# A fused linear-attention and feed-forward kernel rebuilt with tokens on partitions, DMA transposes from the ninth chunk on, and an order written out by a planner

## The chip, the core and the metric

The kernel runs on one core of one Trainium2 chip. The metric is the device time of one launch in microseconds (us). A core has five engines that run their own instruction queues: TensorE (PE, with its weight loads shown apart as PEld), VectorE (DVE), ScalarE (ACT), GpSimd (POOL) and SyncE (SP, which here only issues transfers). Sixteen DMA engines move data. PSUM is the memory that TensorE writes; SBUF is the working memory, 128 partitions wide.

## The reference

Four inputs `r, k, v, w` have shape (4 batches, 8 heads, 768 steps, 48 channels); `u` is (8, 48). For each batch and head a 48 x 48 state runs over the steps, and a feed-forward layer of 384 to 2048 to 384 with a leaky ReLU follows on all 3072 tokens:

```
for t in range(S):
    cur   = outer(u * k[t], v[t])
    y[t]  = r[t] @ (state + cur)
    state = w[t][:, None] * state + outer(k[t], v[t])
x = y rearranged to (3072 tokens, 384)
h = x @ w_in                    # 384 x 2048
out = maximum(0.01 * h, h) @ w_out   # 2048 x 384
```

Everything comes and goes in float32; the inputs are 4 x 4.7 MB, the weights 2 x 3.1 MB and the output 4.7 MB.

## The kernel before, in words

The 768 steps of a batch are cut into 6 chunks of 128 tokens, so there are 24 chunks. In a chunk the recurrence is written as matrix products: the logs of `w` are summed along the tokens by a product with a triangular matrix, `r` and `k` are scaled with the exponentials of the sums, scores of all token pairs are formed and masked, and the state is carried from chunk to chunk. Two heads of 48 channels, padded to 64 each, share the 128 partitions: a pair. So a chunk has four pairs.

For each pair (loop over `p`) TensorE transposes `r` and `k` in float32 (L261, L269), forms the log sums with channels on partitions (L277), the scores of each head (L296), and then four products per head into one tile `ytsu` that has the channels on partitions: masked scores times `v` (L313), the `u` term as a product with the identity (L317), the carried state (L325, 64 rows) and the new state's sum (L332, 64 columns). ScalarE takes the exponentials (L285), VectorE scales and masks (L290, L303) and updates the state (L344). GpSimd and VectorE make `dk`, the `u` term's diagonal and `vsc` (L239 to L251). `ytsu` is copied into `xT`, in which each pair fills 112 of 128 rows.

After every third chunk a feed-forward block of 384 tokens is emitted (`mlp_block`): 16 groups of 4 products, one per pair, into `hp` (L149; two buffers), a copy on ScalarE (L157) and the leaky ReLU on VectorE (L159); then three sums of 16 products into `op` (L171), a copy and the store (L180). `w` is loaded per batch (L191), `r, k, v` per chunk (L212 to L220), all from SP; the weights come as casting transfers from GpSimd's queue (L128 to L135). The order on each engine is that of a tile scheduler, which works blocks and later chunks into one another.

Of the kernel before, what the change touches and what calls it, by code (L numbers as in the profile page):

```python
# [12 lines left out]
AX = mybir.AxisListType  # L13


@with_exitstack
def kernel(
# [11 lines left out]
    nc = tc.nc  # L29
    B, H, S, D = r.shape  # L30
    L = 128
    assert S % L == 0
    C = S // L
    assert H % 2 == 0
    NPAIR = H // 2
    assert D <= 48
    NH = H * D
    NT = NPAIR
    KROWS = 64 + D
    FF = moe_w_in.shape[1]  # L40
    assert FF % 128 == 0
    NFT = FF // 128
    NOUT = moe_w_out.shape[1]
    NTOK = B * S
    MB = 384
    assert S % MB == 0, "sequence must be multiple of mlp block"
    MBC = MB // L

    const = ctx.enter_context(tc.tile_pool(name="const", bufs=1))
    wpool = ctx.enter_context(tc.tile_pool(name="wpool", bufs=1))  # L50
    xtpool = ctx.enter_context(tc.tile_pool(name="xtpool", bufs=1))
    wbpool = ctx.enter_context(tc.tile_pool(name="wbpool", bufs=2))
    natpool = ctx.enter_context(tc.tile_pool(name="natpool", bufs=5))
    slabpool = ctx.enter_context(tc.tile_pool(name="slabpool", bufs=3))
    pairpool = ctx.enter_context(tc.tile_pool(name="pairpool", bufs=8))
    statepool = ctx.enter_context(tc.tile_pool(name="statepool", bufs=2))
    mlppool = ctx.enter_context(tc.tile_pool(name="mlppool", bufs=3))
    gtpool = ctx.enter_context(tc.tile_pool(name="gtpool", bufs=20))
    psum = ctx.enter_context(tc.tile_pool(name="psum", bufs=1, space=bass.MemoryType.PSUM))
    psum2 = ctx.enter_context(tc.tile_pool(name="psum2", bufs=2, space=bass.MemoryType.PSUM))  # L60

    ident_f = const.tile([128, 128], F32, name="ident_f")
    make_identity(nc, ident_f)
    ident_b = const.tile([128, 128], BF16, name="ident_b")
    make_identity(nc, ident_b)

    tcomb = const.tile([128, 256], BF16, name="tcomb")
    nc.gpsimd.memset(tcomb[:, 0:128], 1.0)
    nc.gpsimd.affine_select(
        out=tcomb[:, 0:128],  # L70
        in_=tcomb[:, 0:128],
        compare_op=ALU.is_gt,
        fill=0.0,
        base=0,
        pattern=[[1, 128]],
        channel_multiplier=-1,
    )
    nc.gpsimd.memset(tcomb[:, 128:256], -1.0)
    nc.gpsimd.affine_select(
        out=tcomb[:, 128:256],  # L80
# [41 lines left out]
    def load_weights():  # L122
        if weights_loaded[0]:
            return
# [263 lines left out]
```

## Time and profile before

| | us |
|---|---|
| median of 2 runs (390.86 to 392.42) | 391.64 |
| span of the profiled execution, first to last instruction | 385.2 |
| TensorE busy in the span | 337.2 (88%) |
| VectorE, ScalarE, GpSimd busy | 219.8, 161.4, 107.8 |

The profile is that of one execution, whose own time is its span of 385.2 us and what lies around it; no launch time is given for it, so the 6.4 us between its span and the median of the runs are taken for what lies around it. Busy times are those of a span, and a matmul's mean time is its latency: matmuls are pipelined, so a mean can be longer than the distance from one to the next.

### The profile page before, as it was taken

The page shows a single profiled execution, that of the slowest core. Times are in us where ns is not written, and L with a number is a line of the kernel's source. Part 1 is how long each engine was busy: PE and PEld are TensorE (multiplying, and loading weights), DVE is VectorE, ACT ScalarE, POOL GpSimd, SP SyncE. Part 2 cuts the span into 40 slices and gives each one's busy share as a digit, 9 for nine tenths or more (in the row PEclk, how much of TensorE's full clock was granted, in tenths as well). Part 3 has the DMA queues.
Part 4 walks back from the last instruction along what each step waited for, and adds up shares of the span by engine and source line. Part 5 has one row for each costly group of instructions (what it writes and reads, how often), then busy time and mean ns, then how long its engine had stood idle before and what let it go on. Part 6 is the DMA issues. An engine that isn't in the chain of part 4 may idle for free.

```text
span 385.2 us, 6034 instructions
## 1 busy us (share of the span) xinstructions
PE 337.2 (88%) x2136; PEld 187.8 (49%) x2136; DVE 219.8 (57%) x662; ACT 161.4 (42%) x382; POOL 107.8 (28%) x177
## 2 busy tenths in 40 slices
PE   0455169999999999999999999999999999999886
PEld 0232034455555555556555555555555655555343
DVE  0434045448656884767568837675588457724450
ACT  1535012343375633454486433542375235512341
POOL 5893055141152431234144303331331011000000
PEclk9999999999987999999999999999999999998699
DMA  7999999131532225212323233222220100010001
GB/s 159 176 205 227 217 166 167 15 64 20 128 57 54 39 57 115 48 21 53 96 42 58 57 93 60 41 43 82 43 41 3 62 2 0 2 61 3 0 0 63
DMA packets 87295, 27.33 MB, mean 71 GB/s; under 512 B 75489, under 2 KB 86881, under 8 KB 87265
## 3 DMA queue, kind: packets, MB, share of 16 engines
q1 hardware_dynamic: 84688, 23.80, 31.9%
q0 software_dynamic: 2576, 3.15, 4.8%
q8 instruction: 17, 0.28, 0.3%
q14 instruction: 14, 0.11, 0.1%
HBM read 25.36 MB, written 4.72 MB: 78 GB/s over the span
## 4 chain that ended last, share of the span: by engine, by line
PE 79%; SPq 7%; DMA 5%; DVE 5%; ACT 2%; issue 1%
PE hp L149 24%; PE op L171 16%; PE ytsu L325 7%; PE ytsu L332 6%; PE ytsu L313 6%; PE trcs L261 5%; PE mt L296 4%; DMA w_nat<-in_w_dram 4%; SPq L212 4%; PE trcs L269 3%; PE trcs L277 3%; PE ytsu L317 3%; DVE gt L159 2%; SPq L191 2%; PE esu_ps L227 1%; DVE vsc L251 1%
## 5 line engine op out<-in xcount | busy, mean ns | idle before, releaser
L149 PE MATMUL hp<-xT,w_in_b 112*128 112x384 bf16 x512 | 112.5, 347 | 8.6 <-DVE gt L159 7.0
L159 DVE SCALAR_TENSOR_TENSOR gt<-hp,hs 128x384 bf16<-128x384 f32 x128 | 70.1, 554 | 29.6 <-ACT hs L157 28.3
L157 ACT CAST hs<-hp 128x384 bf16<-128x384 f32 x122 | 58.3, 480 | 53.7 <-PE hp L149 52.3
L149 PEld LDWEIGHTS <-w_in_b 112*128 112x128 bf16 x512 | 50.2, 102 | 41.6 <-issue 18.7
L303 DVE TENSOR_TENSOR mtm<-mt,maskb 128x128 bf16<-128x128 f32 x192 | 51.2, 286 | 27.8 <-PE mt L296 27.1
L171 PE MATMUL op<-w_out_b,gt 128*128 128x384 bf16 x384 | 63.7, 326 | 0.4 <-DVE gt L159 0.4
L285 ACT ACTIVATE ef<-trcs 128x256 f32<-128x256 f32 x96 | 36.2, 384 | 47.6 <-PE trcs L277 45.3
L171 PEld LDWEIGHTS <-gt 128*128 128x128 bf16 x384 | 37.6, 98 | 25.0 <-issue 0.6
L313 PE MATMUL ytsu<-mtm,nat_v 128*64 128x128 bf16 x192 | 47.0, 255 | 1.3 <-DVE mtm L303 1.3
L239 POOL TENSOR_TENSOR dk<-nat_kf,esu 128x512 bf16<-128x512 f32 x24 | 27.8, 1157 | 71.7 <-ACT esu L235 71.3
L185 ACT CAST xT<-ytsu 128x128 bf16<-128x128 f32 x88 | 23.4, 266 | 51.0 <-PE ytsu L332 50.3
L261 PE MATMUL trcs<-ident_f,nat_rf 128*128 128x128 f32 x96 | 32.5, 338 | 13.1 <-DMA nat_rf<-in_r_dram 9.7
L317 PE MATMUL ytsu<-ident_b,vsc 128*64 128x128 bf16 x192 | 43.6, 236 | 0.0
L290 DVE TENSOR_TENSOR rka<-trcs,ef 128x256 bf16<-128x256 f32 x96 | 39.0, 408 | 4.7 <-ACT ef L285 4.7
L332 PE MATMUL ytsu<-nat_v,dk 128*64 128x64 bf16 x192 | 40.8, 222 | 0.0
L325 PE MATMUL ytsu<-rka,s_new 64*64 64x128 bf16 x160 | 40.3, 252 | 0.0
L313 PEld LDWEIGHTS <-nat_v 128*64 128x64 bf16 x192 | 20.2, 110 | 36.8 <-issue 28.8
L296 PE MATMUL mt<-rka 48*128 48x128 bf16 x192 | 28.4, 236 | 8.0 <-DVE rka L290 8.0
L241 POOL TENSOR_TENSOR t<-nat_rf,ukb 128x384 f32<-128x384 f32 x24 | 25.2, 1051 | 32.4 <-DMA nat_rf<-in_r_dram 32.3
L179 ACT COPY osb<-op 128x384 f32<-128x384 f32 x24 | 11.5, 479 | 52.5 <-PE op L171 52.5
L344 DVE SCALAR_TENSOR_TENSOR s_new<-s_new,atot,ytsu 128x64 bf16<-128x64 bf16 x80 | 21.9, 277 | 18.8 <-ACT xT L185 18.2
L251 DVE TENSOR_TENSOR vsc<-nat_vf,diag 128x512 bf16<-128x512 f32 x24 | 22.9, 956 | 14.3 <-PE ytsu L317 14.2
(47 smaller groups left out, 323.0 us busy)
## 6 DMA issues: line engine op xcount, KB each, us to landing
nat_rf<-in_r_dram SPq DMA_DIRECT2D x24, 192.0 KB, 3.2
nat_kf<-in_k_dram SPq DMA_DIRECT2D x24, 192.0 KB, 3.6
nat_vf<-in_v_dram SPq DMA_DIRECT2D x24, 192.0 KB, 2.9
out_dram<-osb SPq DMA_DIRECT2D x24, 192.0 KB, 1.9
w_in_b<-in_moe_w_in_dram POOLq DMA_DIRECT2D x8, 192.0 KB, 8.9
w_out_b<-in_moe_w_out_dram POOLq DMA_DIRECT2D x1, 1536.0 KB, 20.6
ukb<-in_u_dram SPq DMA_DIRECT2D x1, 192.0 KB, 3.6
w_nat<-in_w_dram SPq DMA_DIRECT2D x4, 0.2 KB, 16.3
```

The costliest lines, as they stand in the source:

```text
L149: nc.tensor.matmul(hp[:], lhsT=w_in_b[0:KROWS, t, j * 128 : (j + 1) * 128], rhs=xT[0:KROWS, t, T0 : T0 + MB], start=(t == 0), stop=(t == N ...
L157: nc.any.tensor_copy(out=hs[:], in_=hp[:])
L159: nc.vector.scalar_tensor_tensor(out=gt[:], in0=hp[:], scalar=0.01, in1=hs[:], op0=ALU.mult, op1=ALU.max,)
L171: nc.tensor.matmul(op[:], lhsT=gts[j][:, tsub * 128 : (tsub + 1) * 128], rhs=w_out_b[:, j, :], start=(j == 0), stop=(j == NFT - 1),)
L261: nc.tensor.matmul(trcs[:, 0:128], lhsT=nat_rf[:, hA : hA + 2, :].rearrange("p h d -> p (h d)"), rhs=ident_f[:], is_transpose=True, start= ...
L290: nc.vector.tensor_tensor(out=rka[:], in0=trcs[:, 0:256], in1=ef[:, 0:256], op=ALU.mult)
L296: nc.tensor.matmul(mt[:], lhsT=rka[r0 : r0 + D, 128:256], rhs=rka[r0 : r0 + D, 0:128], start=True, stop=True,)
L303: nc.vector.tensor_tensor(out=mtm[:, hi * 128 : (hi + 1) * 128], in0=mt[:], in1=maskb[:], op=ALU.mult,)
L313: nc.tensor.matmul(yap, lhsT=nat_v[:, hd, :], rhs=mtm[:, hi * 128 : (hi + 1) * 128], start=True, stop=False,)
L317: nc.tensor.matmul(yap, lhsT=vsc[:, hd, :], rhs=ident_b[:], start=False, stop=(s_prev is None),)
L325: nc.tensor.matmul(yap, lhsT=s_prev[r0 : r0 + 64, :], rhs=rka[r0 : r0 + 64, 0:128], start=False, stop=True,)
L332: nc.tensor.matmul(ytsu[r0 : r0 + 64, 128:192], lhsT=dk[:, hd, :], rhs=nat_v[:, hd, :], start=True, stop=True,)
```

## The change

The program is written anew. Tokens are on the partitions up to the output of a chunk; the feed-forward input is packed.

- **Recurrence.** A chunk is worked as a whole, not by pairs. One product (L332 of the changed kernel) gives the log sums of all heads with tokens on partitions; `ci`, `er`, `ek` and the scaled `rk` (r and k side by side, bf16, heads padded to 64) are made in 384 columns each. `rk` is then transposed to `rkT`: in chunks 0 to 7 by 8 bf16 products with the identity and two copies (L385 to L396), from chunk 8 on by one transposing transfer on SP (L402). Scores are 8 products of 48 rows (L471), masked by two VectorE operations of 512 columns (L494). The output `yp` has tokens on partitions: 4 products of the carried state for two heads at once (L522, 96 columns) and 8 of the masked scores (L526, 48 columns). The `u` term is no product any more: it is a GpSimd operation (L423) and an addition (L537). The state's sums are 4 products (L482). `y` is transposed into `xT` in 3 pieces of 128 rows: by products and a copy in chunks 0 to 7 (L547), by one transposing transfer from chunk 8 on (L559).
- **Chunk decay.** The factor for the carried state is made in chunks 1 to 7 by 4 products of one column (L337) and an exponential (L435). From chunk 8 on, row 0 of `er` goes to a scratch row in DRAM (L443), comes back spread over the partitions as 128 x 4 single values (L448), and VectorE takes the reciprocal (L453).
- **Feed-forward.** Blocks are of one chunk, 128 tokens. The 384 channels fill 3 full tiles of 128 rows: 48 products of 128 columns per chunk (L579), in groups of 12 into one `hp` tile of 512 columns (two of them), one leaky ReLU on ScalarE per group (L613), 16 products of 384 columns into the one `op` tile (L631), a copy on VectorE (L642) and the store (L646).
- **Weights** are loaded as float32 by SP in 8 pieces of 0.79 MB behind the first chunks' inputs, and cast by VectorE and ScalarE (L250 to L275).
- **Order.** `Plan` takes every step with an engine, a duration, its dependencies and a priority, and lists the steps by the start times that it finds; the program is emitted in this order on each engine. The recurrence's priorities are 10 per chunk, those of the feed-forward products 1000 and more, so feed-forward products stand where no step of the recurrence was ready.

```diff
-            for p in range(NPAIR):
-                ... (transposes, log sums, scores, four products per head, copies)
-            if (c + 1) % MBC == 0:
-                q = (b * S + (c + 1 - MBC) * L) // MB
-                mlp_block(q)
+    APE = 8
+    NPE = 8
+    LEAD = 3
+    AHEAD = 5
+    WEIGHTS = [(1, 4)] * 4 + [(3, 24)] * 4
+    hp_r = ring("hp", 2, [128, 512], F32, psum)
+    op_r = ring("op", 1, [128, DM], F32, psum)
...
+        for n in range(NCH):
...
+            for src, use in ((w, wn), (k, kn), (r, rn), (v, vn)):
+                def load(src=src, use=use, b=b, t0=t0):
+                    nc.sync.dma_start(
+                        out=use.t, in_=src[b, :, t0 : t0 + L, :].rearrange("h p d -> p h d")
+                    )
...
+            if n < NPE:
+                def tpose(rk=rk, trv=trv):
+                    for g in range(2 * NP):
+                        nc.tensor.transpose(
...
+            else:
+                s_T = [step(
+                    "SP", 0.6,
+                    lambda rk=rk, rkT=rkT: nc.sync.dma_start_transpose(
+                        out=rkT.t[:], in_=rk.t[:].rearrange("p a h d -> p (a h d)")),
...
+                    s_row = step(
+                        "SP", 0.45,
+                        lambda ad=ad, er=er: nc.sync.dma_start(
+                            out=ad.t[:], in_=er.t[0:1].rearrange("o h d -> o (h d)")),
...
+                    s_sp = step(
+                        "SP", 0.45,
+                        lambda ad=ad, a_in=a_in: nc.sync.dma_start(
+                            out=a_in.t[:], in_=ad.t[:].rearrange("o (p q) -> q (o p)", p=NP)),
...
+            def scores(rkT=rkT, se=se, so=so):
+                for p in range(NP):
+                    for par, sc in enumerate((se, so)):
+                        q0 = 64 * par
+                        nc.tensor.matmul(
+                            sc.t[:, p, :], lhsT=rkT.t[q0 : q0 + D, NP + p, :],
+                            rhs=rkT.t[q0 : q0 + D, p, :], start=True, stop=True, skip_group_check=True)
...
+                xt_steps.append(step(
+                    "SP", 0.6,
+                    lambda y=y, col=col: nc.sync.dma_start_transpose(
+                        out=xT[:, :, col : col + L], in_=y.t[:].rearrange("p h d -> p (h d)")),
...
+                def up(hp, j=j, J=J, N=N, c0=c0):
+                    for a in range(J):
+                        for t in range(KT):
+                            nc.tensor.matmul(
+                                hp.t[:, a * N : (a + 1) * N],
+                                lhsT=w_in_b[:, t, (j + a) * 128 : (j + a + 1) * 128],
+                                rhs=xT[:, t, c0 : c0 + N], start=(a == 0 and t == 0),
+                                stop=(t == KT - 1), skip_group_check=True)
...
+        for i in plan.order():
+            plan.fn[i]()
```

What the change does to the queues is seen in the order of the instructions. On TensorE before, the second head's products of a pair stand like this, each with its own weight load (`s_new` is the carried state, `dk` the decayed k):

```order
L317 LDWEIGHTS vsc
L317 MATMUL ytsu<-ident_b,vsc 64x128
L325 LDWEIGHTS s_new
L325 MATMUL ytsu<-rka,s_new 64x128
L332 LDWEIGHTS dk
L332 MATMUL ytsu<-nat_v,dk 64x64
```

In the changed kernel the same place of TensorE's queue, in chunk 12, holds the end of the state's sums and the scores, alternately for the upper and the lower half of the rows:

```order
L482 LDWEIGHTS rk_91
L482 MATMUL pp_150<-vb_99,rk_91 128x96
L471 LDWEIGHTS rkT_94
L471 MATMUL se_147<-rkT_94 128x128
L471 LDWEIGHTS rkT_94
L471 MATMUL so_148<-rkT_94 128x128
```

Between two such pieces stand the feed-forward groups, first products of 128 columns and then products of 384, each with a weight load of 128 columns:

```order
L579 LDWEIGHTS w_in_b
L579 MATMUL hp_144<-xT,w_in_b 128x128
L579 LDWEIGHTS w_in_b
L579 MATMUL hp_144<-xT,w_in_b 128x128
L631 LDWEIGHTS g_130
L631 MATMUL op_145<-w_out_b,g_130 128x384
L631 LDWEIGHTS g_130
L631 MATMUL op_145<-w_out_b,g_130 128x384
```

The products with 64 rows and those with the identity are gone from the steady part; the feed-forward's first products are 48 per chunk with a third of the columns each.

On SP's queue before, past the start, there are only loads and stores:

```order
L212 DMA nat_rf<-in_r_dram 128x8x48
L216 DMA nat_kf<-in_k_dram 128x8x48
L180 DMA out_dram<-osb 128x384
L220 DMA nat_vf<-in_v_dram 128x8x48
L180 DMA out_dram<-osb 128x384 x2
```

In the changed kernel the queue holds from chunk 8 on, per chunk, four loads, one store, the two transposing transfers and the two of the decay:

```order
L297 DMA in_74<-in_r_dram 128x8x48
L443 DMA ad_140<-er_87 1x512
L559 DMA_TRANSPOSE xT<-y_126 128x3x128
L297 DMA in_74<-in_v_dram 128x8x48
L402 DMA_TRANSPOSE rkT_96<-rk_92 128x8x128
L297 DMA in_75<-in_w_dram 128x8x48
L297 DMA in_75<-in_k_dram 128x8x48
L443 DMA ad_141<-er_85 1x512
L448 DMA a_118<-ad_140 128x4x1
```

Each transposing transfer stands in line with the loads of later chunks, and waits there for the VectorE operation that makes its source.

## Rows read from the trace of the kernel before

**Rows 1.** Page, parts 1 and 2: busy us; busy tenths in 40 slices.

```profile
PE 337.2 (88%) x2136; PEld 187.8 (49%) x2136; DVE 219.8 (57%) x662; ACT 161.4 (42%) x382; POOL 107.8 (28%) x177
PE   0455169999999999999999999999999999999886
```

**Rows 2.** Page, part 4: chain that ended last, share by engine and by line.

```profile
PE 79%; SPq 7%; DMA 5%; DVE 5%; ACT 2%; issue 1%
PE hp L149 24%; PE op L171 16%; PE ytsu L325 7%; PE ytsu L332 6%; PE ytsu L313 6%; PE trcs L261 5%; PE mt L296 4%; DMA w_nat<-in_w_dram 4%; SPq L212 4%; PE trcs L269 3%; PE trcs L277 3%; PE ytsu L317 3%; DVE gt L159 2%; SPq L191 2%; PE esu_ps L227 1%; DVE vsc L251 1%
```

**Rows 3.** Groups by line, forms apart, TensorE: count, busy us, mean ns, idle before.

```profile
L149 PE MATMUL hp<-xT,w_in_b 112*128 112x384 bf16 x512 | 112.5, 347 | 8.6 <-DVE gt L159 7.0 <-ACT xT L185 1.4
L171 PE MATMUL op<-w_out_b,gt 128*128 128x384 bf16 x384 | 63.7, 326 | 0.4 <-DVE gt L159 0.4
L171 PEld LDWEIGHTS <-gt 128*128 128x128 bf16 x384 | 37.6, 98 | 25.0 <-issue 0.6
```

**Rows 4.** Timeline of TensorE at 203 us: start us, us, engine, line, tiles, count.

```profile
203.30 1.47 PE L149 MATMUL hp<-xT,w_in_b 112*128 112x384 bf16 x8
204.70 0.25 PE L313 MATMUL ytsu<-mtm,nat_v 128*64 128x128 bf16 x2
204.78 0.23 PE L317 MATMUL ytsu<-ident_b,vsc 128*64 128x128 bf16 x2
204.83 0.20 PE L332 MATMUL ytsu<-nat_v,dk 128*64 128x64 bf16 x2
204.97 0.23 PE L296 MATMUL mt<-rka 48*128 48x128 bf16 x2
205.13 0.33 PE L261 MATMUL trcs<-ident_f,nat_rf 128*128 128x128 f32 x1
```

**Rows 5.** Groups by line, forms apart: the other engines' operations.

```profile
L159 DVE SCALAR_TENSOR_TENSOR gt<-hp,hs 128x384 bf16<-128x384 f32 x128 | 70.1, 554 | 29.6 <-ACT hs L157 28.3
L303 DVE TENSOR_TENSOR mtm<-mt,maskb 128x128 bf16<-128x128 f32 x192 | 51.2, 286 | 27.8 <-PE mt L296 27.1
L290 DVE TENSOR_TENSOR rka<-trcs,ef 128x256 bf16<-128x256 f32 x96 | 39.0, 408 | 4.7 <-ACT ef L285 4.7
L251 DVE TENSOR_TENSOR vsc<-nat_vf,diag 128x512 bf16<-128x512 f32 x24 | 22.9, 956 | 14.3 <-PE ytsu L317 14.2
...
L235 ACT ACTIVATE esu<-esu_ps 128x512 bf16<-128x512 f32 x24 | 14.3, 596 | 2.3 <-PE esu_ps L227 2.0
...
L241 POOL TENSOR_TENSOR t<-nat_rf,ukb 128x384 f32<-128x384 f32 x24 | 25.2, 1051 | 32.4 <-DMA nat_rf<-in_r_dram 32.3
```

**Rows 6.** Page, parts 3 and 6: queues (packets, MB, share); issues (KB, us to landing).

```profile
q1 hardware_dynamic: 84688, 23.80, 31.9%
q0 software_dynamic: 2576, 3.15, 4.8%
nat_rf<-in_r_dram SPq DMA_DIRECT2D x24, 192.0 KB, 3.2
...
out_dram<-osb SPq DMA_DIRECT2D x24, 192.0 KB, 1.9
...
w_nat<-in_w_dram SPq DMA_DIRECT2D x4, 0.2 KB, 16.3
```

**Rows 7.** Busy us by stretch: PE, PEld, DVE, ACT, POOL, PEclk, DMA share, GB/s.

```profile
20.00:30.00 10.00, 4.45 (x26) 2.73 (x25) 2.60 (x6) 3.82 (x9) 9.96 (x20) 1.00 1.10 205
150.00:200.00 50.00, 48.81 (x334) 27.84 (x333) 33.92 (x107) 26.04 (x58) 15.85 (x24) 1.00 0.29 59
```

**Rows 8.** Timeline of TensorE at 71 us, the same eight products.

```profile
71.64 2.72 PE L149 MATMUL hp<-xT,w_in_b 112*128 112x384 bf16 x8
```

**Rows 9.** Timeline of TensorE in the last block.

```profile
363.84 1.57 PE L149 MATMUL hp<-xT,w_in_b 112*128 112x384 bf16 x8 [0.40 <-DVE gt L159]
```

**Rows 10.** Timeline of the end, ScalarE and SP's queue.

```profile
381.69 0.48 ACT L179 COPY osb<-op 128x384 f32<-128x384 f32 x1 [2.12 <-PE op L171]
382.20 0.33 SPq L180 DMA_DIRECT2D out_dram<-osb  x1
```

More of the change, by code (lines that the diff above doesn't have):

```diff
@@ L1 @@
+import heapq
 from contextlib import ExitStack
@@ L6 @@
 from concourse._compat import with_exitstack
-from concourse.masks import make_identity
 F32 = mybir.dt.float32
@@ new lines, with __init__, take @@
+class Ring:
+    def __init__(self, tiles):
+        self.tiles = tiles
+        self.steps = [[] for _ in tiles]
+        self.n = -1
+    def take(self):
+        self.n += 1
+        k = self.n % len(self.tiles)
+        old, self.steps[k] = self.steps[k], []
+        return Use(self.tiles[k], old, self.steps[k])
+class View:
+    def __init__(self, use, t):
+        self.t, self.old, self.steps = t, use.old, use.steps
+class Use:
+    def __init__(self, t, old, steps):
+        self.t, self.old, self.steps = t, old, steps
@@ L51 @@
[L51 to L57, printed above, removed]
@@ L69 @@
[L69 to L80, printed above, removed]
-        in_=tcomb[:, 128:256],
-        compare_op=ALU.is_ge,
-        fill=0.0,
-        base=0,
-        pattern=[[1, 128]],
-        channel_multiplier=-1,
-    )
@@ new lines @@
+    NCH = B * C
+    NP = H // 2
+    DM = H * D
+    KT = DM // 128
+    FF = moe_w_in.shape[1]
+    NJ = FF // 128
+    assert S % L == 0 and H % 2 == 0 and D <= 64 and DM % 128 == 0 and FF % 512 == 0
+    NQ = FF // 512
+    APE = 8
[3 more added lines that the diff above has]
+    WEIGHTS = [(1, 4)] * 4 + [(3, 24)] * 4
+    blocks = [1] * NCH
+    assert sum(blocks) == NCH
+    pool = ctx.enter_context(tc.tile_pool(name="pool", bufs=1))
+    psum = ctx.enter_context(tc.tile_pool(name="psum", bufs=1, space=bass.MemoryType.PSUM))
@@ new lines, in ring @@
+    def ring(name, count, shape, dtype, where=None):
+        return Ring([(where or pool).tile(shape, dtype, name=f"{name}{i}") for i in range(count)])
+    trev = pool.tile([128, 128], BF16, name="trev")
+    maskb = pool.tile([128, 128], BF16, name="maskb")
+    ident = pool.tile([128, 128], BF16, name="ident")
+    ones = pool.tile([128, 1], BF16, name="ones")
+    ub = pool.tile([128, DM], F32, name="ub")
+    w_in_b = pool.tile([128, KT, FF], BF16, name="w_in_b")
+    w_out_b = pool.tile([128, NJ, DM], BF16, name="w_out_b")
@@ new lines @@
+    xT = pool.tile([128, KT, NCH * L], BF16, name="xT")
+    in_r = ring("in", 11, [128, 1536], F32)
+    lw_r = ring("lw", 3, [128, H, 64], BF16)
+    ci_r = ring("ci", 2, [128, H, D], F32)
+    er_r = ring("er", 3, [128, H, 64], F32)
+    ek_r = ring("ek", 2, [128, H, D], F32)
+    rk_r = ring("rk", 4, [128, 2, H, 64], BF16)
+    rkT_r = ring("rkT", 4, [128, 2 * NP, 128], BF16)
+    vb_r = ring("vb", 6, [128, H, D], BF16)
+    ru_r = ring("ru", 2, [128, H, D], F32)
+    dg_r = ring("dg", 3, [128, H], F32)
```

716 lines of the change are left out of this document (443 added, 273 removed).

## The prediction

> **What bounds the kernel now.** I read the page's busy shares first, then the chain of waits, then TensorE's groups and its timeline, and last what the other engines and the transfers cost. TensorE is busy 88% of the span, and after the start its slices are full [rows 1]. The chain that ended last runs through TensorE for 79% of the span [rows 2]: the feed-forward products take 40%, and the recurrence's products nearly as much. So the kernel is bound by TensorE's time, and what counts is how much of that time is useful columns. For the feed-forward it nearly all is: eight products of 384 columns take 1.47 us [rows 4], and the 384 of L171 are busy 63.7 us, 0.166 us each [rows 3], although one takes 326 ns from start to end. L149 is busy 112.5 us for 512 products, 0.22 us each: the reader is to see here that the same products also run at half the pace, 2.72 us for eight at 71 us [rows 8], the lower of the clock's two levels (1.2 GHz) by their time, whatever the clock column of that stretch says. What is left of TensorE's 337.2 us is 337.2 - 112.5 - 63.7 = 161 us for the recurrence. That is where most can be lost or won.
>
> **The change, part by part.** The sum is made against the profiled span of 385.2 us plus the 6.4 us outside it, so against 391.6 us, the median of the runs.
>
> *TensorE, removed:* all of its 337 us; the program is new. *Added, feed-forward:* 24 x 48 = 1152 products of 128 columns in place of 512 of 384, a quarter fewer columns, since three full tiles of rows replace four of 112. The price of one such product with its own weight load of 128 columns is in no row. From below: a third of 0.16 us, 0.053 us. From above: the load alone, 98 ns [rows 3], if nothing hid it. The nearest row is a dense run of short products: six (640 columns, six loads) start from 204.70 to 204.97 us, 0.045 us each [rows 4], so loads hide well there, though these loads have 64 columns. I take 0.060 us: 69 us (61 to 113). The second products are unchanged: 384 x 0.166 = 64 us.
>
> The Trainium skill (TensorE: Matmul & The Clock Gate, "Back-to-back issue gap") says that a stream of weight load and matmul pairs is sustained at about 81 ns per pair for 128 columns; by it this term would be 93 us and my sum 249 us. The trace has no dense run of such pairs; its short products are faster than that.
>
> *Added, recurrence:* 192 score products of 48 rows, alternating between the two halves of the rows. Two such (L296) take 0.16 us before the next product starts, from 204.97 to 205.13 [rows 4]: 0.08 us each, 15 us. 24 log sums of 384 columns at 0.166: 4 us. All the rest are products of 1 to 128 columns with a load each: 80 (L482), 80 (L522), 192 (L526), 64 and 24 transposes of the first eight chunks, 24 of one column: 464 x 0.060 = 28 us. Together 47 us in place of 161. TensorE's sum is 69 + 64 + 47 = 180 us, or 7.5 us per chunk.
>
> *Other engines, per chunk, in the same 7.5 us.* VectorE: five operations of 384 columns like L159 (554 ns; the reduction among them), two scalings like L251 in proportion (956 x 384/512 = 720 ns, which includes its waiting beside GpSimd), two masks of 512 columns (286 + 384 x (408 - 286)/128 = 650 ns) and two state additions of 192 (350 ns) [rows 5]: 6.2 us. ScalarE: four leaky ReLUs of 512 columns like L235 (596 ns) and three passes of 384 like the copy at the end (0.48 us) [rows 5, 10]: 3.8 us. GpSimd: three operations at 1.05 us and two smaller: 4.2 to 5.3 us [rows 5]. All lie beside TensorE's work, VectorE only just. If TensorE were faster than I think, VectorE would be the next bound.
>
> *Transfers, per chunk.* Inputs and output, 0.98 MB, at 59 GB/s for a share of 0.29 [rows 7], so 203 GB/s for a full share: 4.8 us. The transposing transfers are in no row. From below: as 1408 rows of 256 bytes at the mean price of a packet, 31.9% x 385.2 x 16 / 84688 = 23.2 ns [rows 6], over 16 engines: 2.0 us per chunk, 0.19 us per 128 x 128 block. From above: if each needed the 16.3 us that the slowest transfer here takes to land [rows 6]. I take the lower end for the engines' time and the 3.2 us in which a load of `r` lands [rows 6], since the rows moved are as long as those. The decay's 512 single values: 512 x 23.2 / 16 = 0.7 us. Sum 7.6 us against TensorE's 7.5 from chunk 8 on; the loads run five chunks ahead, so I charge nothing. Without that cover it would cost little, but a longer queue makes each transposing transfer late.
>
> *The moved waits.* In the order, TensorE has some 9 us of its own work between a chunk's log sum and its scores (chunk 12: seven groups of L579, four or five of L631 and small ones). Before the transfer can start, `ci`, `ek` and the scaled k take about 2.3 us on two engines; 6.5 us are left for issue and landing of `rkT`. Between the output of a chunk and its first feed-forward group stand about 7 us for `y` and its transfer. So at 3.2 us of landing nothing is late. The scratch row's two transfers, 1.9 us or more each as a store lands [rows 6], fit in the same 9 us. On SP a transfer that waits for its source holds back the loads behind it, which have five chunks of lead.
>
> *Start.* Ahead of the first product of L631 come, on SP's queue, three chunks' inputs and `u` (2.56 MB at the 205 GB/s of [rows 7], 12.5 us), all of w_in and the first quarter of w_out (3.93 MB). The weights' rate now is 6.29 MB read in 4.8% of 385.2 us [rows 6], 340 GB/s: 11.6 us. With 2 us to begin that is 26 us, and TensorE has 9.5 us of work until then: 16.5 us lost. Chunk 3's inputs come behind the rest of w_out, at 37 us, some 5 us after TensorE has run out of other work, and the slow clock of the beginning leaves 1.5 us. Start: 23 us. Bounds: with weights at 205 GB/s 12 us more; with the clock low until 60 us, as before, 17 more.
>
> *Stalls.* In the middle of the span now TensorE is idle 2.4% [rows 7]; in the last block, where it does nothing but wait for its two `hp` buffers, 0.40 of 1.97 us, 20% [rows 9]. The changed order has two `hp` buffers too, but L631 groups between most of them, and only one `op` buffer, which waits for VectorE's copy. I take 7% of 180 us, 12.5 us, nearer the lower end (4 to 36).
>
> *End.* A copy of 0.48, an issue of 0.33 [rows 10], landing 1.9 us [rows 6]: 3 us.
>
> Sum: 180 + 23 + 12.5 + 3 + 6.4 = **225 us**.
>
> **The rivals.**
>
> *Loads not hidden.* If weight loads of 128 columns hide only behind longer products, 1152 + 352 products cost up to 98 instead of 60 ns: 57 us more, 282 us; half hidden, 253. For it: L171's products hide their loads behind 384 columns, and no row shows a dense run of 128 with 128. Against it: the six of [rows 4]. The page of the Trainium skill cited above lies in this case. Chance 0.19.
>
> *Late transposes.* If transposing transfers land as `w_nat` does, in 16.3 us, they are 10 us past TensorE's cover; with three chunks under way that is 3.3 us per chunk, for 16 chunks 52 us, and as much again if `y`'s is late too: 277 to 329 us. For it: one queue carries nine transfers per chunk, and the engines' 7.6 us are as much as TensorE has. Against it: loads of much the same size land in 3.2 us [rows 6]. Chance 0.16.
>
> *Slower than before.* The transposing transfers are served one after the other and their own price sets the pace of the last 16 chunks. At p us per 128 x 128 block a chunk takes 11 p + 5.5 us, and the whole 23 + 8 x 7.5 + 16 x (11 p + 5.5) + 9.4 us. It passes 399.5 us (2% over the median) from p = 1.24 us on. Moved in pieces of 16 values, 32 bytes, a block is 1024 packets at 23.2 ns over 16 engines, p = 1.48 us: 441 us. For it: values of two bytes must change places, and a packet costs time whatever it holds. Against it: row by row p is 0.19. Chance 0.03.
>
> The Trainium skill (VectorE: DVE Perf Modes, "The three transpose paths") gives 1309 ns for a 128 x 128 transpose by DMA and 390 ns by TensorE, which speaks against moving it; taken as p, its figure would give 411 us. No row here shows a transposing transfer.
>
> *Better than the sum.* Products at 0.053 us, hardly a stall: 190 to 203 us. Chance 0.06.
>
> **How the numbers follow.** The sum's own case has 0.56, from 203 us (products at 0.054, stalls 4 us) to 245 us (clock low for long, or weights at 205 GB/s). With loads not hidden 245 to 282, with late transposes 245 to 390. The range 203 to 275 us leaves out 0.06 below, and above it 0.02 of the loads' case, 0.09 of the late transposes and 0.03: 0.20. Two per cent, 8 us, is about what a measurement of this kernel can tell from no change. Only the slower case and the very end of the late transposes come near it: faster 0.96, within 2% 0.01, slower 0.03.
>
> **What would show it.** In the changed profile: TensorE near 180 us busy of a span of about 219; L579 at 0.06 us each by start times; VectorE at 150 us; the first L631 at 26 us; transposing transfers landing in about 3 us; idle time of L471 before `rkT` small. The prediction is wrong if L579's groups of 12 take 1.2 us, if L471 or L579 wait for transfers over 2 us per chunk, or if SP's queue is busy all the time.

## The result and the profile after

The changed kernel takes **228.53 us** (228.19 to 228.86 in two runs) against 391.64 before: a ratio of 0.5828, 95% interval 0.5783 to 0.5873. The forecast was 225 us in a range of 203 to 275. The forecast case came, but its sum is right partly by errors that cancel; most of what follows is on that. Both runs of the kernel before (390.86 and 392.42 us) stand at the level of its slower runs beside the later experiments (390 us and more), and the experiments' ratios are taken against its faster ones there (383 to 387 us), by which the changed kernel's own would be about 0.594 (228.53 / 385) and not 0.5828. So the experiments are compared with the changed kernel by their times, and with each other by their ratios. The changed kernel was not measured again beside them, and a difference of one or two per cent from its two runs can't be told from none.

The changed kernel's page, first parts, answers to [rows 1]: TensorE is busy for 178 us where it was for 337, and of its 40 slices only those of the last quarter are nearly all full. The clock row falls in two places (slices 5 and 6, then 18 and 19) and a little in a third.

```profile
span 227.1 us, 5592 instructions
PE 178.0 (78%) x2216; PEld 136.4 (60%) x2216; DVE 153.0 (67%) x297; ACT 102.2 (45%) x199; POOL 97.1 (43%) x125
...
PE   0437679987989996529887998589887989998983
...
PEclk9999659999999999956999999999998899999998
DMA  7999999899999999963999598998988144325101
...
q1 hardware_dynamic: 138124, 35.92, 83.7%
...
PE 27%; DMA 17%; DVE 7%; issue 2%; ACT 2%; SPq 2%; POOL 1%; POOLq 0%
PE hp L579 13%; PE op L631 10%; DMA rkT<-rk 7%; DMA a<-ad 7%; DVE rk L373 2%; DMA xT<-y 2%; DMA in<-in_v_dram 1%; DVE ci L347 1%; DVE m L494 1%; PE se L471 1%; PE pp L482 1%; ACT er L354 1%; DVE s L510 1%; PE yp L522 1%; ACT g L613 1%
```

The chain (the last two rows) answers to [rows 2]. TensorE's part of it fell from 79% to 27%; transfers now make 17% of it, and two of them, the transposing one of r and k and the one that brings the decay back from its row in DRAM, 7% each. These are what the change put on the path from the ninth chunk on. The DMA row (mean busy share of the transfer engines) is nearly full for three quarters of the span; before, the whole queue's share was 31.9% [rows 6].

Next the groups of part 5 that answer to [rows 3], with VectorE's dearer scaling (busy us, mean ns of one, then idle time just before it). A group's busy time counts the end of each burst over again, beside the next one's start, so the price of a product is read from start times below.

```profile
L579 PE MATMUL hp<-xT,w_in_b 128*128 128x128 bf16 x1152 | 82.9, 227 | 2.6 <-DMA xT<-y 1.7
...
L631 PE MATMUL op<-w_out_b,g 128*128 128x384 bf16 x384 | 77.6, 331 | 3.2 <-DVE o L642 3.1
...
L373 DVE TENSOR_TENSOR rk<-in,ek 128x384 bf16<-128x384 f32 x24 | 20.9, 870 | 0.2
...
L471 PE MATMUL se<-rkT 48*128 48x128 bf16 x96 | 10.3, 232 | 9.9 <-DMA rkT<-rk 8.4
```

TensorE's timeline in a dense stretch answers to [rows 4] (start, length, engine, line, operation, tile; a row can hold several products).

```profile
134.42 0.83 PE L579 MATMUL hp<-xT,w_in_b 128*128 128x128 bf16 x12
135.09 0.81 PE L631 MATMUL op<-w_out_b,g 128*128 128x384 bf16 x4
135.74 0.83 PE L579 MATMUL hp<-xT,w_in_b 128*128 128x128 bf16 x12
...
138.72 0.23 PE L471 MATMUL se<-rkT 48*128 48x128 bf16 x1 [0.83 <-DMA rkT<-rk]
138.72 0.23 PE L471 MATMUL so<-rkT 48*128 48x128 bf16 x1
138.79 0.22 PE L471 MATMUL se<-rkT 48*128 48x128 bf16 x1
...
139.05 0.82 PE L631 MATMUL op<-w_out_b,g 128*128 128x384 bf16 x4
```

From 134.42 to 135.09 twelve products of 128 columns, each with a weight load of its own, take 0.67 us: **0.0557 us each**. The four of L631 take 0.65, 0.162 each. The score products of the two row halves start at the same instant, a pair every 0.06 us; eight of them take 0.33 us until the next line starts, 0.041 each.

What TensorE waited for (total us, times, longest) comes from the view of waits, and the transfers' landing times from the view of DMA issues (KB each where known, median us from issue to landing).

```profile
PE se L471 <- DMA rkT<-rk: 8.4, 7, 3.3
PE so L547 <- DVE y L537: 6.4, 4, 2.9
PE pp L482 <- DVE rk L373: 4.7, 4, 1.7
PE yp L522 <- POOL sb L462: 4.6, 5, 1.7
```

```profile
rkT<-rk SPq DMA_TRANSPOSE x16, 4.0
xT<-y SPq DMA_TRANSPOSE x16, 2.3
...
a<-ad SPq DMA_DIRECT2D x14, 2.0 KB, 3.1
```

The largest wait is where the switch happens. Here are SyncE's queue and then TensorE from 94 us on.

```profile
93.28 0.69 SPq L297 DMA_DIRECT2D in<-in_v_dram  x1
94.07 2.29 SPq L402 DMA_TRANSPOSE rkT<-rk  x1
96.45 0.53 SPq L448 DMA_DIRECT2D a<-ad  x1
...
98.55 6.56 SPq L559 DMA_TRANSPOSE xT<-y  x2
```

```profile
94.73 0.33 PE L482 MATMUL pp<-vb,rk 128*128 128x96 bf16 x4
98.34 0.28 PE L471 MATMUL se<-rkT 48*128 48x128 bf16 x1 [3.28 <-DMA rkT<-rk]
...
100.27 0.48 PE L522 MATMUL yp<-sb,rkT 128*128 128x96 bf16 x4 [1.31 <-POOL sb L462]
...
102.42 1.44 PE L579 MATMUL hp<-xT,w_in_b 128*128 128x128 bf16 x12 [1.36 <-DMA xT<-y]
```

The last operation of VectorE that can have made this transfer's source stands here:

```profile
86.65 1.35 DVE L373 TENSOR_TENSOR rk<-in,ek 128x384 bf16<-128x384 f32 x1
```

So the source was ready at 88.00. The transposing transfer is issued only at 94.07, behind four loads, an output and transfers of the decay, holds SyncE's queue for 2.29 us, and its tile lets the scores start at 98.34; from 98.55 on the two transposing transfers of y stand behind all this. TensorE stands for 3.28, 1.31 and 1.36 us, and the twelve products at 102.42 take until 103.66, nearly twice the 0.67 us: the lower clock.

### The profile page after: what moved, and what is told of

Read it like the earlier page. It is cut to its first block, busy times and chain, and to the rows that moved or that the text cites. A ratio compares the mean times of both kernels' runs of the same rounds, so it can differ in the third digit from the quotient of the medians.

```text
span 227.1 us, 5592 instructions
## 1 busy us (share of the span) xinstructions
PE 178.0 (78%) x2216; PEld 136.4 (60%) x2216; DVE 153.0 (67%) x297; ACT 102.2 (45%) x199; POOL 97.1 (43%) x125
## 2 busy tenths in 40 slices
DMA packets 138150, 36.27 MB, mean 160 GB/s; under 512 B 131326, under 2 KB 136574, under 8 KB 138124
## 3 DMA queue, kind: packets, MB, share of 16 engines
q1 hardware_dynamic: 138124, 35.92, 83.7%
## 4 chain that ended last, share of the span: by engine, by line
PE 27%; DMA 17%; DVE 7%; issue 2%; ACT 2%; SPq 2%; POOL 1%; POOLq 0%
PE hp L579 13%; PE op L631 10%; DMA rkT<-rk 7%; DMA a<-ad 7%; DVE rk L373 2%; DMA xT<-y 2%; DMA in<-in_v_dram 1%; DVE ci L347 1%; DVE m L494 1%; PE se L471 1%; PE pp L482 1%; ACT er L354 1%; DVE s L510 1%; PE yp L522 1%; ACT g L613 1%
## 5 line engine op out<-in xcount | busy, mean ns | idle before, releaser
L613 ACT ACTIVATE g<-hp 128x512 bf16<-128x512 f32 x96 | 56.9, 595 | 83.2 <-PE hp L579 82.6
L579 PE MATMUL hp<-xT,w_in_b 128*128 128x128 bf16 x1152 | 82.9, 227 | 2.6 <-DMA xT<-y 1.7
L579 PEld LDWEIGHTS <-w_in_b 128*128 128x128 bf16 x1152 | 74.4, 102 | 11.3 <-issue 3.7
L631 PE MATMUL op<-w_out_b,g 128*128 128x384 bf16 x384 | 77.6, 331 | 3.2 <-DVE o L642 3.1
L631 PEld LDWEIGHTS <-g 128*128 128x128 bf16 x384 | 34.3, 98 | 20.2 <-issue 4.6
L462 POOL TENSOR_TENSOR sb<-s,a 64x192 bf16<-64x192 f32 x40 | 21.5, 538 | 54.9 <-DVE a L453 24.5
L411 POOL TENSOR_TENSOR ru<-in,ub 128x384 f32<-128x384 f32 x24 | 25.5, 1065 | 30.4 <-DMA in<-in_r_dram 22.9
L423 POOL TENSOR_TENSOR vs<-in,dg 128x384 f32<-128x384 f32 x24 | 21.3, 888 | 19.8 <-DVE dg L419 6.0
L415 POOL TENSOR_TENSOR ru<-ru,in 128x384 f32<-128x384 f32 x24 | 26.1, 1091 | 1.6
L642 DVE COPY o<-op 128x384 f32<-128x384 f32 x24 | 13.3, 553 | 17.7 <-PE op L631 17.2
L373 DVE TENSOR_TENSOR rk<-in,ek 128x384 bf16<-128x384 f32 x24 | 20.9, 870 | 0.2
L494 DVE TENSOR_TENSOR m<-se,maskb 128x512 bf16<-128x512 f32 x24 | 16.4, 684 | 6.4 <-PE so L471 6.1
L471 PE MATMUL se<-rkT 48*128 48x128 bf16 x96 | 10.3, 232 | 9.9 <-DMA rkT<-rk 8.4
L494 DVE TENSOR_TENSOR m<-so,maskb 128x512 bf16<-128x512 f32 x24 | 16.2, 676 | 0.0
L471 PEld LDWEIGHTS <-rkT 48*128 48x128 bf16 x192 | 6.1, 100 | 15.0 <-DMA rkT<-rk 10.7
L537 DVE TENSOR_TENSOR y<-yp,vs 128x384 bf16<-128x384 f32 x24 | 13.2, 550 | 2.7 <-PE yp L526 2.4
L360 ACT ACTIVATE ek<-ci 128x384 f32<-128x384 f32 x24 | 12.5, 519 | 4.2 <-DVE ci L347 4.0
```

What stands on the lines that cost most here:

```text
L373: lambda rk=rk, kn=kn, ek=ek: nc.vector.tensor_tensor(out=rk.t[:, 1, :, 0:D], in0=kn.t, in1=ek.t[:], op=ALU.mult),
L411: lambda ru=ru, rn=rn: nc.gpsimd.tensor_tensor(out=ru.t[:], in0=rn.t, in1=ubv, op=ALU.mult),
L415: lambda ru=ru, kn=kn: nc.gpsimd.tensor_tensor(out=ru.t[:], in0=ru.t[:], in1=kn.t, op=ALU.mult),
L423: lambda vs=vs, vn=vn, dg=dg: nc.gpsimd.tensor_tensor(out=vs.t[:], in0=vn.t, in1=dg.t[:].unsqueeze(2).to_broadcast([128, H, D]), op=ALU.mult),
L462: lambda sb=sb, s_in=s_in, a_in=a_in, q0=q0, half=half: nc.gpsimd.tensor_tensor(out=sb.t[q0 : q0 + 64, :, half, :], in0=s_in.t[q0 : q0 + 6 ...
L471: nc.tensor.matmul(sc.t[:, p, :], lhsT=rkT.t[q0 : q0 + D, NP + p, :], rhs=rkT.t[q0 : q0 + D, p, :], start=True, stop=True, skip_group_chec ...
```

## The experiments

**Which of the two moved things costs what.** Three kernels undo the two parts from the ninth chunk on: the constants APE and NPE say for how many chunks the decay and the transposes of r, k and y stay on TensorE.

```
e1_pe_all               APE = 24   NPE = 24
e2_decay_dma_only       APE = 8    NPE = 24
e3_transpose_dma_only   APE = 24   NPE = 8
```

> Transposes and chunk decay by TensorE in all 24 chunks (no transposing transfer, no scratch row). Theory A (TensorE's work sets the pace, the transfers lie beside it, and only the switch at chunk 8 stalled): TensorE gets 16 x 11 products of 128 columns more at 0.056 us, 10 us, and VectorE 0.4 us and ScalarE 1.1 us more per chunk; the stall of about 8 us at 94 to 102 us and the slow clock behind it go: 222 to 232 us against 228.5. Theory B (the transfer queue sets the pace, its engines are busy 84% of the span): without 16 x 11 blocks and 14 x 512 single values the kernel is faster, 205 to 216 us.

Measured: ratio 0.5689 [0.565, 0.5728], 219.01 us: between the bands of A and B.

> Transposes by TensorE in all chunks, the decay through the scratch row from chunk 8 on. A: as the kernel without either, within 2 us of it (222 to 232 us): the scratch row has cover. B: the 7168 single values still lie on the queue, so it lies half way between the run without both and the changed kernel (210 to 222 us).

Measured: **0.5605 [0.5569, 0.564]**, 215.66 us, 5.6% under the changed kernel (215.66 / 228.53 = 0.944) and 1.5% under e1.

> Transposes by transfer from chunk 8 on, the decay by TensorE in all chunks. A: like the changed kernel, 226 to 230 us, with TensorE's waits for rkT as before. A third theory, C (the scratch row's two transfers behind one another, 3.1 us to land, hold SP and the carried state): faster by 4 to 10 us, 218 to 224.

Measured: 0.5802 [0.573, 0.5873], 224.31 us, between A's band and C's. So the transposes by DMA cost time: e1, which differs from e3 only in them, is 2% faster, and e2 is 5.6% faster than the changed kernel. The decay's row costs nothing where the queue has no transposes in it: e2, which differs from e1 only in that row, is the faster of the two. Beside the transposes it is not settled. The changed kernel has 4.6 us of waits before L522 for the scaled state, and e3's view of waits lists none there, but 224.31 against 228.53 is 1.8%, within what two runs can tell. The windows from 110 to 160 us, of the changed kernel and then of e2 (busy us of TensorE first, the clock third from the end), show where:

```profile
110.00:160.00 50.00, 41.84 (x544) 31.58 (x543) 37.30 (x70) 21.88 (x45) 24.52 (x29) 1.00 1.03 167
```

```profile
110.00:160.00 50.00, 48.73 (x687) 38.79 (x686) 41.61 (x88) 31.85 (x63) 24.61 (x31) 1.00 0.63 125
```

At the same full clock TensorE is busy 6.9 of 50 us more. Part of that is the transposes it does itself; 687 products stand against 544, so it also gets further.

**Is it the load on the transfer engines?** e4 reads the inputs in rows of 1536 bytes in place of 192, so that its values are other than the reference's.

```
-  out=use.t, in_=src[b, :, t0 : t0 + L, :].rearrange("h p d -> p h d")
+  out=use.t.rearrange("p h d -> p (h d)"),
+  in_=src[b].rearrange("h (a i) d -> (h a) (i d)", i=8)[t0 : t0 + L, :],
```

> The four loads of a chunk take rows of 1536 bytes (eight steps of one head, so other values than the reference's) in place of 192 bytes; the same bytes, the same instructions and order, an eighth of the packets. A: only the start gains, since chunk 1's inputs come sooner: 220 to 228 us. B: the queue's engines lose over half of their busy time, and the kernel becomes 15 to 25 us faster: 203 to 213 us.

Measured: 0.5738 [0.5693, 0.5783], 220.49 us, 3.5% under the changed kernel: within A's band and above B's. The reason that A gave does not hold, though. By 35 us TensorE has worked on 184 products where the changed kernel has 167, by 200 us on 2078 where it has 1953, so most of the gain comes behind the start. The queue's packets fall from 138124 to 52108 and its share from 83.7% to 60.6%. Here are the hold of SyncE's queue (ns, min, median and max) in the changed kernel, then in e4, and e4's wait for `rkT` (8.4 us, 7 times, in the changed kernel; e4's line numbers are higher by one).

```profile
L402 SPq DMA_TRANSPOSE rkT<-rk x16: 1232/1780/3320, 80.7 to 202.9; - x16
```

```profile
L403 SPq DMA_TRANSPOSE rkT<-rk x16: 1231/1239/2583, 75.0 to 193.3; - x16
PE se L472 <- DMA rkT<-rk: 3.1, 6, 1.1
```

The tile still lands after 3.9 us, but its issue holds the queue for less, and so do the loads. Added up from SyncE's timeline, issues hold the queue for 44 of the 50 us from 110 us on in the changed kernel, 37 in e4 and 21 in e2. So the load on the engines is a good part of what makes the tiles late, and it acts through the queue: each issue holds it longer, and a tile's turn comes later. No run gave the transposing transfers a queue of their own, so how the lateness divides between the queue's order and that load stays open.

**Is it the planner's order?** e11 gives the planner the measured prices of the transposing transfers.

```
-                    "SP", 0.6,
+                    "SP", 1.8,
...
-                    P0, reads=[rk], writes=[rkT], deps=[s_r, s_k], wire=1.0)]
+                    P0, reads=[rk], writes=[rkT], deps=[s_r, s_k], wire=2.3)]
...
-                    "SP", 0.6,
+                    "SP", 1.2,
```

> The changed kernel with the prices in its planner set to what the trace shows: 1.8 us of SyncE for a transposing transfer of r and k where 0.6 stood, 1.2 for one of y, and 2.3 instead of 1.0 us of transfer for r and k; instructions and sizes stay, their order changes. Theory A (the waits from the ninth chunk on come from an order that asks for the transposed tiles too early): idle before L471 falls from 8.4 to under 4 us, the stretch from 80 to 110 us gains 3 us of TensorE's time or more, and the whole takes 4 to 8 us less than the changed kernel: a ratio to the kernel before of 0.562 to 0.573. Theory B (the one queue is late whatever the order): within 2 us of the changed kernel, a ratio of 0.578 to 0.588.

Measured: 0.5903 [0.5847, 0.5959], 227.82 us, 0.7 under the changed kernel; A falls, and B's consequence came (within 2 us of the changed kernel). In the profile, which is of its longest execution (230.2 us) and so only a hint, the wait before L471 goes from 8.4 to 4.9 us, in this near A, but the one of L579 for `xT` grows from 1.7 to 6.2. That fits a lateness that moves along the same queue; one other order does not show that every order is late.

**Is it the clock that falls in the wait?** e13 fills the longest waits with products that write the same values again.

```
-            def scores(rkT=rkT, se=se, so=so):
-                for p in range(NP):
+            def scores(rkT=rkT, se=se, so=so, times=(4 if n == 10 else 1)):
+                for p in [*range(NP)] * times:
...
-                def sums(pp=pp, rk=rk, vb=vb):
-                    for p in range(NP):
+                def sums(pp=pp, rk=rk, vb=vb, times=(18 if n == 9 else 1)):
+                    for p in [*range(NP)] * times:
```

> The changed kernel with TensorE kept at work in its longest wait: chunk 9's four state products (L482) eighteen times in place of once, in the 3.28 us before chunk 10's scores, and these scores four times, in the 1.31 us before L522; they write the same values again, and the order of all else stays. 68 products at 0.042 us and 24 at 0.041 are 3.9 us of TensorE's time in 4.6 us of waits, so by themselves they cost nothing. Theory A (the granted clock fell there because TensorE stood idle): the clock of the stretch from 94 to 106 us, 0.50 to 0.76 in the changed kernel, stays over 0.9, the work behind it is done some 2 to 4 us earlier, and the ratio to the kernel before goes from 0.583 to 0.573 to 0.578. Theory B (it falls for another reason, as it does in the kernel before while TensorE works without a gap): the clock falls all the same, the fillers take twice as long and run over the wait, and the ratio is 0.582 to 0.592.

Measured: 0.5881 [0.5844, 0.5918], 226.66 us, 1.9 under the changed kernel. Windows of the changed kernel, then of e13 (clock third from the end):

```profile
94.00:98.00 4.00, 0.80 (x16) 0.62 (x15) 2.39 (x6) 0.00 (x0) 2.10 (x4) 0.76 1.19 174
98.00:102.00 4.00, 1.41 (x20) 1.15 (x21) 1.46 (x3) 0.00 (x0) 1.93 (x3) 0.50 0.53 128
102.00:106.00 4.00, 3.58 (x41) 3.58 (x41) 2.90 (x8) 1.51 (x3) 1.83 (x3) 0.50 0.12 25
```

```profile
94.00:98.00 4.00, 3.22 (x72) 3.07 (x71) 2.06 (x4) 0.00 (x0) 2.62 (x3) 1.00 1.13 185
98.00:102.00 4.00, 2.27 (x56) 2.10 (x57) 1.93 (x6) 0.00 (x0) 1.20 (x3) 1.00 0.36 80
102.00:106.00 4.00, 3.40 (x60) 2.98 (x57) 3.87 (x10) 3.03 (x7) 2.67 (x4) 1.00 0.14 29
```

A's first half holds: with TensorE at work the clock stays at its higher level, in that stretch and behind it (mean of the span 0.977 in place of 0.944). B falls with it. Of A's second half little is left: 1.9 us is just under the 2 to 4 that it asked for, and within what two runs of the changed kernel can tell. By the clock record e13 spends about 15 us less at the lower level, (1 - 0.944) / 0.5 x 227.1 - (1 - 0.977) / 0.5 x 225.0, which would be worth 7.5 us if TensorE's speed set the pace all through it. The products run faster and then wait longer; in the 50 us from 110 TensorE is busy 40.07 us. So, by this estimate, the lower clock was mostly paid out of waiting.

**Is TensorE the pace once the transposes are back on it?** e6 is e2 with a fourth product in each group of L579 (row tile 2 twice, so the sums are other than the reference's): 384 products more.

```
-  for t in range(KT):
+  for i, t in enumerate((0, 1, 2, 2)):
```

> On e2: a fourth product in each group of the feed-forward's first part (tile 2 a second time, so the values are not the reference's), 64 per chunk in place of 48, which is what four tiles of rows, unpacked as before, would need. If TensorE's time sets the pace now: 384 x 0.056 = 21 us more than e2, 17 to 23. Rival (chain and transfers set the pace, TensorE has room): under 8 us more.

Measured: 0.5946 [0.5908, 0.5984], 228.72 us against e2's 215.66: 13.1 us more, between the theories. At 0.0557 us, 384 products are 21.4 us, so about 8 found room in e2 (its idle time goes from 32.2 to 26.6 us) and 13 went into the time. TensorE sets most of e2's pace, not all.

**Do the weight loads hide?** e5 is e2 with two chunks to a feed-forward block: half as many loads in front of products of 256 columns.

```
-  blocks = [1] * NCH
+  blocks = [2] * (NCH // 2)
```

> On the kernel with all transposes by TensorE (e2): blocks of two chunks, so 24 products of 256 columns per chunk in place of 48 of 128, half the weight loads for the same columns. If loads hide (12 products of 128 columns with a load each started 0.056 us apart in the changed kernel's trace): a product of 256 takes 0.107 to 0.11 us, TensorE's sum stays within 3 us, and the time is that of e2 or up to 8 us more, since a block waits for two chunks at the start and leaves two at the end. Rival (loads cost something in the stream): 5 us or more below e2.

```profile
142.25 0.82 PE L579 MATMUL hp<-xT,w_in_b 128*128 128x256 bf16 x6
142.90 0.34 PE L547 MATMUL so<-ident,y 128*128 128x128 bf16 x3
```

Six products of 256 columns take 0.65 us where twelve of 128 took 0.67: halving the loads gives 3%, so the loads are hidden. But the whole takes 0.6152 [0.6123, 0.6181], 236.61 us, 21 us more than e2, of which I had expected 8 at most. TensorE is idle for longer (43.36 of the 50 us from 110 busy, against 48.73); that this is because a block waits for two chunks is argued and not shown.

**The start.** e7 is e2 with the first weights loaded behind more of the inputs; e12 is e7 with measured prices in the planner (among them 0.0557 us a product) and four chunks of lead in place of three.

```
-  WEIGHTS = [(1, 4)] * 4 + [(3, 24)] * 4
+  WEIGHTS = [(1, 11)] * 4 + [(3, 24)] * 4      (e7; e12 also: LEAD = 4)
```

> On e2: chunk 1's four loads stand ahead of w_in on SP's queue. If the start is bound by the order of arrival (the first product of L631 stood at 32 us behind chunk 1's recurrence, whose loads came after w_in): chunk 1's recurrence is done while w_in loads, L631 begins at 27 to 30 us, and the kernel is 2 to 5 us faster than e2. Rival (the start is bound by the bytes alone, w_in only comes 4 us later): no change, or 1 to 3 us slower.

Measured: **0.5556 [0.5516, 0.5596]**, 213.56 us, the fastest version: 6.6% under the changed kernel and 1% under e2, whose interval overlaps with its own, so what shows the start's gain is the timeline. Its rows, of the changed kernel and of e7, show the first L631:

```profile
32.75 1.49 PE L631 MATMUL op<-w_out_b,g 128*128 128x384 bf16 x4
```

```profile
28.72 0.81 PE L631 MATMUL op<-w_out_b,g 128*128 128x384 bf16 x4 [0.36 <-DVE w_out_b L273]
```

It starts 4 us earlier and only now behind w_out's conversion, and at nearly twice the pace.

> The fastest version so far (no transfers for r, k and the decay, first weights behind chunk 1's inputs, ratio 0.5556) with true prices in its planner: 1.2 us of SyncE for the transposing transfer of y, 0.84 us for VectorE's two scalings, 0.0557 us for a product of 128 columns, and the recurrence allowed four chunks ahead of the feed-forward in place of three. Theory: its TensorE is busy in nearly all of the stretch from 110 us on, so what is left is the start and the stretch from 35 to 80 us (37.5 us busy of 45); 0 to 4 us less, a ratio of 0.545 to 0.556. Rival: a fourth chunk ahead takes TensorE time from the feed-forward at the start and gives the copies in the middle more waits: 1 to 4 us more, a ratio of 0.558 to 0.566.

Measured: 0.5609 [0.5596, 0.5623], the rival's band. A single wait of L522 for the scaled state, 5.8 us, stands in its profile where e7 has none of that length; which of its changes brought it was not tested.

**What the removed recurrence cost.** e10 is the kernel before without its 160 products with the carried state (L325), e9 without its 192 products with the identity (L317); the removed lines are shown abridged.

```
e10:  - nc.tensor.matmul(yap, lhsT=s_prev[r0 : r0 + 64, :], rhs=rka[r0 : r0 + 64, 0:128], ...)
e9:   - nc.tensor.matmul(yap, lhsT=vsc[:, hd, :], rhs=ident_b[:], ...)
```

> The kernel before without the 160 products of the carried state (L325, 64 rows; the output lacks that term). By its trace a product of 64 rows takes 0.26 us out of the stream (L317 to L325 to L332 start 0.14 and 0.17 us apart, L317 to L332 alone 0.05). If the recurrence's products were TensorE time on the path: 160 x 0.26 = 41 us less, 340 to 358 us. Rival (the recurrence before was held by VectorE and ScalarE, TensorE only looked full): under 15 us less, above 372 us.

Measured: 0.8885 [0.883, 0.8939], 43 us less, 0.27 us a product. The recurrence's short products were on the path. But not all of the 43 us is the products' own price, as the first eight of L149 together in e10 and then, in the kernel before, the first four at the full pace show:

```profile
66.69 1.47 PE L149 MATMUL hp<-xT,w_in_b 112*128 112x384 bf16 x8
```

```profile
84.04 0.81 PE L149 MATMUL hp<-xT,w_in_b 112*128 112x384 bf16 x4
```

The kernel before is still at the lower pace at 71.64 us [rows 8]. With some 18 us less at it, of which half is lost time, about 9 of the 43 us are the clock's; that leaves about 0.21 us a product, by estimate. Even that is far more than the 0.0557 us of a product with all rows and as many columns.

> The kernel before without its 192 products with the identity (L317), so its output lacks the intra-chunk term of the values that they add; everything else stays. Theory (each such product is TensorE time at its spacing in the timeline, 0.05 to 0.08 us): 10 to 15 us less, a ratio to the kernel before of 0.96 to 0.975. Rival (the gap of 0.14 us up to the next product of 64 rows belongs to it): about 27 us less, a ratio near 0.93. Second rival (they stand in time in which TensorE waits anyway): under 4 us, a ratio over 0.99.

Measured: **1.0395 [1.0322, 1.0468]**: less work, and 15 us slower. All three expectations fall. The windows from 100 to 150 us of the kernel before, then of e9, and a row of e9's timeline:

```profile
100.00:150.00 50.00, 49.47 (x339) 28.35 (x336) 33.17 (x105) 26.34 (x63) 15.84 (x25) 0.93 0.33 72
```

```profile
100.00:150.00 50.00, 48.53 (x241) 24.71 (x240) 29.14 (x94) 23.39 (x54) 12.04 (x20) 0.69 0.23 48
```

```profile
121.56 2.74 PE L149 MATMUL hp<-xT,w_in_b 112*128 112x384 bf16 x8
```

TensorE is busy as fully as before, but the granted clock is 0.69, and eight products take 2.74 us in place of 1.47 [rows 4]. Over the span the clock is 0.893 in place of 0.978. With levels of 1.2 and 2.4 GHz that is (1 - 0.893) / 0.5 x 399.4 = 85 us at the lower one against (1 - 0.978) / 0.5 x 385.2 = 17. The record leaves out the start, where the column says 1.00 and products take twice as long [rows 8]; e9 comes to the full pace there some 8 us sooner (four of L149 in 0.82 us from 75.88 us). So about 60 us more at the lower level, in which work takes nearly twice its time, and some 30 us lost. 30 - 15 leaves 15 us gained by the 192 products, 0.08 us each, the upper end of what was expected of them. That is an estimate; that the clock took the gain is read from the rows and not tested. Why it falls in a stretch in which TensorE hardly stands still was not settled.

## Why the prediction was right, point by point

**The bound was read rightly.** TensorE's time set the kernel before, and the recurrence was where most could be won. e10's 43 us and the recurrence's part of the changed kernel (below) bear that out.

**TensorE's sum: 180 us forecast, 178.0 busy, but not by the terms.** At the full clock L579 is 1152 x 0.0557 = 64 us (69 forecast, at 0.060) and L631 384 x 0.162 = 62 (64). The recurrence was the mis-sized term: 47 us forecast. Measured by start times the scores are 192 x 0.041 = 8 us (15: the row they were priced by was a lone pair before another kind of product, not one in a stream), the log sums 24 x 0.16 = 4, and the 464 others about 18 (28). Together 30. So the full-clock sum is 64 + 62 + 30 = 156, and about 22 us of the 178 are work at the lower clock and the ends of bursts before waits. TensorE is busy at the lower level for 7.3 us from 24.4 to 34.6 us, 5.2 from 96 to 106.2 and 3.4 from 174.6 to 178, and for 9.1 before 21 us, where the clock column says 1.00 but the products of L579 come 0.106 us apart. Half of these 25 us, 12 or 13, is what the clock cost by estimate; the rest is the ends of bursts. The prediction put 1.5 us on the clock. These two errors, 24 us down and 22 up, nearly cancel, which is luck.

**Loads not hidden (0.19): fell.** 0.0557 us is near the lower bound of 0.053, and e5's halved loads change it by 3%. The Trainium skill's 81 ns per pair for 128 columns (TensorE: Matmul & The Clock Gate, "Back-to-back issue gap") does not hold here: the trace disagrees, with twelve pairs in 0.67 us over and over.

**Start: 23 us forecast.** TensorE is idle 17.2 us of the first 35, less than forecast, though L631 began at 32.75 us and not at 26. The step that failed is the order: L631 stood behind chunk 1's recurrence, whose inputs come after w_in, and not behind w_out. e7 moves those inputs ahead and has L631 at 28.72 us.

**Stalls: 12.5 us forecast, the step that was wrong.** From 35 to 218 us TensorE is idle 27.8 us, 15% and not 7. "So at 3.2 us of landing nothing is late" failed. The transposing transfer of r and k lands after 4.0 us and not 3.2, but what matters more was costed at nothing: its issue holds SyncE's queue for 1.78 us in the median and up to 3.32, with loads, outputs and the decay's two transfers in the same queue, which from 87.86 to 98.5 us has no gap over 0.1 us. The transfer is issued late, and the scores wait for it seven times, 8.4 of the 27.8 us. Of the rest, 4.7 us are waits for VectorE's scaling of k and 4.6 for the scaled state, whose decay comes back through the same queue. e2, without the transposing transfers, is 5.6% faster. e4 shows that the engines' load, to which the prediction charged nothing, is a good part of it, since it lengthens the holds; e11 that one other order moves the wait, and e13 that the lower clock beside it costs little. The sign "if SP's queue is busy all the time" nearly came: 44 of the 50 us from 110 us. And the moved tiles of a chunk cost the engines about 2.8 us (last section) where 2.0 were forecast.

**End and outside.** The last windows hold 4.1 us of idle time behind 218 us against 3. Outside the span lie 228.9 - 227.1 = 1.8 us, not 6.4. The kernel before has as much (386.34 us with a span of 384.6 in a later run); the other 4.6 are the distance of its profiled execution from the two runs that it was held against.

**The whole:** work 24 us less, clock and burst ends 22 more, idle 49.1 in place of 38.5, outside 4.6 less: -24 + 22 + 10.6 - 4.6 = +4, and 225 + 4 is the 229 of the profiled execution.

**Late transposes (0.16)** came in part, at a fifth of the price or less: 8.4 us of waits for `rkT` and 1.7 for `xT`, not 52 or more, since landing is 4.0 and 2.3 us and not 16.3. **The slower rival (0.03)** fell: eight blocks in 4.0 us are at most 0.5 us per block of the path, far from 1.24. The Trainium skill's 1309 ns (VectorE: DVE Perf Modes, "The three transpose paths") is likewise not what a block costs in a transfer of eight. But its order of the two paths is borne out: e2 and e1, with the transposes on TensorE, are faster. **Better than the sum (0.06)** did not come, though the product price came near the one that it assumed (0.0557 us for 0.053); what was missing was its "hardly a stall".

**VectorE** was forecast at 150 us and is busy 153.0. L373 takes 870 ns where 720 were forecast, L494 684 where 650.

## What to carry to other kernels

Price a product by the spacing of starts in a dense stretch of the same kind, and check the sum against the clock row before trusting that it fits: a total that agrees can hide two wrong terms. When work moves to a transfer, count the time that its issue holds the queue and what stands ahead of it there, not only its bytes and its landing; that hold grew here with the load on the transfer engines. The transposes cost TensorE about 10 us (16 x 11 products at 0.0557), and the queue's lateness cost more. And what an operation costs by its rows is not what taking it out gives back, if the granted clock changes with the mix of work.

## What the runs showed of the hardware

Taking 192 products out of the kernel before made it 4% slower, with the granted clock at 0.893 in place of 0.978 and TensorE busy 88% of the span in both. In the changed kernel 92 products in two waits kept the clock at 1.00 where it had fallen to 0.50, and the time fell by only 1.9 us of 228.5.

Products on the two halves of the rows start at the same instant and cost 0.041 us each in such pairs, less than one of 128 rows and as many columns (0.0557). In the kernel before, taking out products on 64 of the rows, most of which stand between products on all 128, gave back 0.27 us each, or about 0.21 without the clock's share (e10).

The queue of e2, without transposing transfers:

```profile
q1 hardware_dynamic: 114572, 30.15, 67.8%
```

Moving r, k and y by transposing transfers adds 23552 packets to the queue for 16 chunks (138124 against 114572), 1472 per chunk where 1408 rows of 256 bytes are moved (1024 of r and k, 384 of y), and about 2.8 us of the 16 engines' time per chunk: (83.7% x 227.1 - 67.8% x 214.0) / 16. One issue of r and k held SyncE's queue for 1.78 us in the median under that load and for 1.24 in e4, whose engines carried fewer packets.
